# Moving the weight scans' fetches to GpSimd's queue, with five buffers for the last eight, in a four-layer linear-attention and gated-MLP kernel

## The chip, the cores and the metric

The kernel runs on one core of a Trainium2 chip. The metric is the device time of one execution in microseconds (us). Before the change it was 1498.74 us (median of three runs, 1498.54 to 1498.86). All runs named below gave correct results.

## The reference

Layer A is linear attention and layer B a gated MLP without a nonlinearity. The program applies A, B, A, B with the same weights.

```python
def A(x, wqkv, wo):                       # S=2048, D=1024, 32 heads of 32
    q, k, v = split_heads(x @ wqkv)
    phi = lambda t: where(t > 0, t + 1, exp(t)) + 1e-6
    pq, pk = phi(q), phi(k)
    kv, z = einsum("bhsd,bhse->bhde", pk, v), einsum("bhsd->bhd", pk)
    o = einsum("bhqd,bhde->bhqe", pq, kv) / (einsum("bhqd,bhd->bhq", pq, z)[..., None] + 1e-6)
    return merge_heads(o) @ wo

def B(x, w_gate, w_up, w_down):           # F=3584
    return ((x @ w_gate) * (x @ w_up)) @ w_down

x = x + A(layernorm(x)); x = x + B(layernorm(x)); x = x + A(layernorm(x)); x = x + B(layernorm(x))
```

## The kernel before

The kernel computes layer B in float16, so it needs one power-of-two scale per weight matrix. During the first layer A it therefore *scans* `w_gate`, `w_up` and `w_down`: 42 pieces of 512 KB are fetched, and ScalarE squares and sums each (L221). Pieces 0 to 27 are gate and up, and 28 to 41 are down. The first 14 fetches are issued by the sync engine, the other 28 by ScalarE itself, most of them right after the scan that frees their buffer.

```python
scan_a = [K[i][:, j * 2 * D:(j + 1) * 2 * D] for i in (3, 1) for j in range(2)]
scan_b = [W[:, 6 * D:8 * D], K[0][:, HEAD:HEAD + 2 * D]]
scan_c = [K[i][:, HEAD:HEAD + 2 * D] for i in (4, 0)]
# ... cut ...
EARLY, MID = 26, 33
scan_buf = [scan_a[i % 4] for i in range(18)] + [(scan_a + scan_b[:1])[i % 5] for i in range(18, EARLY)]
scan_buf += [scan_b[(i + 1) % 2] for i in range(MID - EARLY)] + [scan_c[i % 2] for i in range(NSCAN - MID)]

def scan_fetch():
    while scanned[1] < scanned[2]:
        i = scanned[1]
        if any(scan_buf[j] is scan_buf[i] for j in range(scanned[0], i)):
            return                                   # buffer not scanned yet
        src, k = scan_src(i)
        (nc.sync if i < 14 else nc.scalar).dma_start(                                        # L213
            out=scan_buf[i].rearrange("p (k n) -> p k n", k=k), in_=src)
        scanned[1] += 1

def scan_step(n=1):
    for _ in range(n):
        i = scanned[0]                                   # cut: the indices of acc
        nc.scalar.activation(out=scan_buf[i], in_=scan_buf[i], func=ACT.Square, accum_out=acc[...])   # L221
        scanned[0] += 1
        # ... cut: loads of wv, and the limit raised to MID ...
        scan_fetch()

def scale_sum(lo, hi):      # VectorE: L230 sums acc into part, L231 copies it to partb
def scale_pow(lo, hi):      # TensorE: one-column matmul with ones (L236); VectorE max; GpSimd power (L238)
def scale_bits(lo, hi):     # VectorE: keep the exponent only
```

The stage with the change is the second half of layer A. Eleven `q` tiles are woven with products `pk^T x` (`xk`). Then come `kv_unit` (L490), five more `q` tiles with `kvo_unit` between them (the products with `wo`, L500), and 16 output tiles (L510, with VectorE's add to `X` at L512). Each slot of the output stage carries *jobs* for the other engines: norms for layer B, the scans left over, the scale chain of `w_down`, and the preparation of layer B's weights.

```python
def kvo_unit(c):
    def run():
        ps = turn("kvo", QP[2:4])
        for n in range(2):
            nc.tensor.matmul(out=ps[:, n, :], lhsT=kvt[:, c, :], rhs=wo[n][:, c, :], start=True, stop=True)
        nc.scalar.activation(out=KVo[c], in_=ps, func=ACT.Copy, scale=rz[:, c:c + 1])
    return run
# ... cut ...
for t in range(XT_):                                  # XT_ = 11
    q_tile(t, li > 0, done=2 * (t < XT_ - 1))
    do(rest[pos[0]:pos[1]])                           # xk products
    # ... cut: z, and the scale chain of gate and up at t = 7, 8, 9 ...
    if t == XT_ - 3:
        load_o()                                      # wo, two halves, sync queue
    scans(0 if t > 8 else 2 - t % 2)
kv_unit()
load_unit(0, 0)
if first_A:
    scanned[2] = NSCAN
    scan_fetch()                                      # the last pieces of w_down: two buffers
q_tile(XT_, True)
# ... cut ...
    job(13, lambda: scale_sum(2, 3))
    job(13, dp[1][0])
    job(17, lambda: scale_pow(2, 3))
    job(19, lambda: scale_bits(2, 3))
    for i in range(2, 11):
        job(i, scans)
    for i, f in enumerate(list(dp[0][1:]) + list(dp[1][1:])):
        job((20, 21, 26, 27)[i], f)                   # dp: prepared w_down, stored to DRAM as WD
```

Of the kernel before, what the change touches and what calls it, by code (L numbers as in the profile page):

```python
# [37 lines left out]
def kernel(  # L38
# [11 lines left out]
    nc = tc.nc  # L50
    P = 128
    S, D = A_x.shape[1], A_x.shape[2]
# [27 lines left out]
    K = [const.tile([P, BLK], BF16, tag=f"K{i}", name=f"K{i}") for i in range(8)]  # L80
# [3 lines left out]
    QP = [QQ[:, 2 * i:2 * i + 2, :] for i in range(4)]  # L84
    WD = dram.tile([7, P, BLK], F16, name="WD")

    HEAD = KD * NB
# [22 lines left out]
    kvt = W[:, 5 * D:6 * D].rearrange("p (c f) -> p c f", f=P)  # L110
    scan_a = [K[i][:, j * 2 * D:(j + 1) * 2 * D] for i in (3, 1) for j in range(2)]
    scan_b = [W[:, 6 * D:8 * D], K[0][:, HEAD:HEAD + 2 * D]]
    scan_c = [K[i][:, HEAD:HEAD + 2 * D] for i in (4, 0)]

    xn_c = {TPG + i: tail(i, 0) for i in range(4)}
    xn_b = [ST[:, t % TPG * D:(t % TPG + 1) * D] for t in range(NT)]
# [8 lines left out]
    def turn(name, bufs):  # L125
        count[name] = count.get(name, -1) + 1
        return bufs[count[name] % len(bufs)]
# [70 lines left out]

    NGU = 2 * NU
    NSCAN = 3 * NU  # L200
    EARLY, MID = 26, 33
    scan_buf = [scan_a[i % 4] for i in range(18)] + [(scan_a + scan_b[:1])[i % 5] for i in range(18, EARLY)]
    scan_buf += [scan_b[(i + 1) % 2] for i in range(MID - EARLY)] + [scan_c[i % 2] for i in range(NSCAN - MID)]
    scanned = [0, 0, 0]

    def scan_fetch():

        while scanned[1] < scanned[2]:
            i = scanned[1]
            if any(scan_buf[j] is scan_buf[i] for j in range(scanned[0], i)):  # L210
                return
            src, k = scan_src(i)
            (nc.sync if i < 14 else nc.scalar).dma_start(out=scan_buf[i].rearrange("p (k n) -> p k n", k=k), in_=src)  # L213
            scanned[1] += 1

    def scan_step(n=1):
# [12 lines left out]
    def scale_sum(lo, hi):  # L229
        nc.vector.tensor_reduce(out=part[:, lo:hi], in_=acc[:, lo:hi, :], axis=AX.X, op=ALU.add)  # L230
        nc.vector.tensor_copy(out=partb[:, lo:hi], in_=part[:, lo:hi])  # L231

    def scale_pow(lo, hi):

        ps = mm_tile()
        nc.tensor.matmul(out=ps[:, lo:hi], lhsT=ones[:], rhs=partb[:, lo:hi], start=True, stop=True)  # L236
        nc.vector.tensor_scalar(out=part[:, lo:hi], in0=ps[:, lo:hi], scalar1=1e-30, scalar2=None, op0=ALU.max)
        nc.gpsimd.tensor_tensor(out=fac[:, lo:hi], in0=part[:, lo:hi], in1=mhalf[:, lo:hi], op=ALU.pow)  # L238
# [30 lines left out]
    def ln_stats(t):  # L269
        bn(t, 0)  # L270
        bn(t, 1)
        moments(t)
# [222 lines left out]
    def kvo_unit(c):  # L495

        def run():
            ps = turn("kvo", QP[2:4])
            for n in range(2):
                nc.tensor.matmul(out=ps[:, n, :], lhsT=kvt[:, c, :], rhs=wo[n][:, c, :], start=True, stop=True)  # L500
            nc.scalar.activation(out=KVo[c], in_=ps, func=ACT.Copy, scale=rz[:, c:c + 1])
        return run
# [181 lines left out]
    def layer_A(li):  # L684
        sks = [sum_unit(t, nc.vector) for t in range(1, NT)]
        first_A = li == 0

        def scans(n=1):
            if first_A:
                scan_step(n)  # L690

        if li == 0:
            def txp(t):
                return lambda: tx_pe(xn_a[t], t)

            def norm(t):
                ln_apply_act(t, xn_a[t])
                tx(xn_a[t], t, t // TPG)

            bn(0, 0)  # L700
            bn(0, 1)
            moments(0)
            bn(1, 0)
            bn(1, 1)
            ln_tx_halves(0, xn_a[0])
            ln_apply(1, xn_a[1])
            ln_stats(2)
            u = k_mm(0, 0, txp(1), KD // 2)
            ln_apply(2, xn_a[2])
            phi(*u)  # L710
            u = k_mm(1, 0, txp(2))
            ln_stats(3)
            bn(4, 0)
            ln_apply(3, xn_a[3])
            bn(4, 1)
            moments(4)
            phi(*u)
            ln_apply(4, xn_a[4])
            tx(xn_a[4], 4, 1)

            units = [(2, 0), (0, 1), (1, 1), (3, 0), (2, 1), (3, 1)]
            units += [(t, n) for t in range(TPG, NT) for n in range(2)]
            ready = []
            for i, (t, n) in enumerate(units):
                if t < TPG:
                    u = k_mm(t, n, txp(3), KD // 2) if i == 1 else k_mm(t, n)
                elif n == 0:
                    u = k_tile(t)
                late = ready
                ready = [4 + (i + 4) // 2 if i > 1 else 5 + i] if i < 2 or (i % 2 == 0 and i <= 18) else []  # L730
                for x in ready:
                    ln_stats(x)
                if t < TPG or n == 0:
                    phi(*u)
                for x in late:
                    norm(x)
                if i == 2:
                    for x in range(3 * TPG, NT):
                        load_x(x)
                if i >= 5 and i % 2:  # L740
                    scanned[2] = (i - 3) // 2 if i < len(units) - 1 else EARLY
                    scan_fetch()
                if 10 <= i <= 28 and i % 2 == 0:
                    scans()
                if t > 10 and n == 1:
                    sks.pop(0)()
            load_qkv(wq, 0)
        else:
            load_qkv(wq, 0)
            load_qkv(wv, 2)  # L750
            count["mm"] = 5
            fill = norm_fill(3, 3, xn_a)
            for t in range(NT):
                phi(*k_tile(t), True)
                do(fill[2 * t:2 * t + 2])
                if t > 0:
                    sks.pop(0)()

        xk = [xk_pair(c) for c in range(KD)]
        first = 3 if first_A else 1  # L760
        for i in range(first):
            xk[i]()
            do(sks[5 * i:5 * i + 5])
            if i == min(2, first - 1):
                z_parts()
            scans(3)
        rest = xk[first:]
        XT_ = 11

        for t in range(XT_):  # L770
            pos = [-(-len(rest) * x // (XT_ - 1)) for x in (t, t + 1)]
            q_tile(t, li > 0, done=2 * (t < XT_ - 1))
            do(rest[pos[0]:pos[1]])
            if t == 0:
                z_unit()
            elif t == 2:
                z_column()
            elif first_A and t == 7:
                scale_sum(0, 2)
            elif first_A and t == 8:  # L780
                scale_pow(0, 2)
            elif first_A and t == 9:
                scale_bits(0, 2)
            if t == XT_ - 3:
                load_o()
            scans(0 if t > 8 else 2 - t % 2)
        kv_unit()
        load_unit(0, 0)
        if first_A:
            scanned[2] = NSCAN  # L790
            scan_fetch()
        q_tile(XT_, True)
        norm = norm_act(0, 0, xn_b, TPG) + norm_act(1, 1, xn_c, 2)
        late = norm[10:]
        jobs = {i: norm[i - 8:i - 7] for i in range(8, 18)}
        for i in range(6):
            jobs[18 + i] = late[len(late) * i // 6:len(late) * (i + 1) // 6]

        def job(i, *f):
            jobs[i] = list(f) + jobs.get(i, [])  # L800

        for i in range(4):
            job(3 + i, prep(0)[i])
        if first_A:
            job(9, dp[0][0])
            job(13, lambda: scale_sum(2, 3))
            job(13, dp[1][0])
            job(17, lambda: scale_pow(2, 3))
            job(19, lambda: scale_bits(2, 3))
            for i in range(2, 11):  # L810
                job(i, scans)
            for i, f in enumerate(list(dp[0][1:]) + list(dp[1][1:])):
                job((20, 21, 26, 27)[i], f)
        job(24, lambda: load_unit(1, 1))
        for i in range(4):
            kvo_ = [kvo_unit(2 * i), kvo_unit(2 * i + 1)]
            q_tile(XT_ + 1 + i, True, kvo_[0:1], kvo_[1:2], 2)
        count["mm"] = 7
        for t in range(NT):
            if t == NT - 2:  # L820
                load_unit(2, 2)
                if first_A:
                    dp[2][0]()
                sums_t[:] = t_fill()
            if t in (7, 10, 13) and not (first_A and t == 10):
                mm_pair()
            out_tile(t)
            if t < 3:
                flush()
                flush()  # L830
            do(jobs.get(2 * t, []))
            do(jobs.get(2 * t + 1, []))
            if t >= NT - 2:
                sums_t.pop(0)()
# [215 lines left out]
```

## Time and profile before

| | before |
|---|---|
| median, first three runs | 1498.74 us |
| TensorE (PE) busy | 1478.4 of 1497.5 us |
| wait of PE for the scale of `w_down` | 3.57 us, then 4 us at a reduced clock |
| wait of ScalarE for the last fetches | 1.38 and 4.33 us |

The profile is of a run of 1499.30 us. PE is busy for 99% of the span, so only its gaps can be won. This is the list of PE's waits between 100 and 260 us. A row reads: engine, line, what it waited for, total us, times, longest.

```profile
PE Q L236 <- DVE partb L231: 3.6, 1, 3.6
PE Q L372 <- DVE W L364: 0.8, 1, 0.8
PE Q L500 <- ACT W L359: 0.4, 1, 0.4
PE Q L510 <- DVE X L512: 0.4, 1, 0.4
PE Q L500 <- DMA TX<-in_A_wo_dram: 0.3, 1, 0.3
```

The first row is the largest. PE's timeline (start, duration, engine, line, operation; in brackets the idle time before it and what ended it) shows it in place:

```profile
217.76 1.67 PE L510 MATMUL Q<-K,K 128*128 128x512 bf16 x7
223.00 0.16 PE L236 MATMUL Q<-partb,ones 128*128 128x1 bf16 x1 [3.57 <-DVE partb L231]
223.03 5.28 PE L510 MATMUL Q<-K,K 128*128 128x512 bf16 x15
```

Fifteen matmuls take 5.28 us after the gap, while seven took 1.67 us before it. The windows table says why. After each window stand its length, the busy time of each engine, and at the end three figures without a count: PE's granted clock, the DMA share and GB/s.

```profile
core 0: us, PE busy (x) PEld busy (x) DVE busy (x) ACT busy (x) POOL busy (x), PEclk, DMA share, GB/s
219.00:223.00 4.00, 0.43 (x3) 0.10 (x1) 0.38 (x3) 4.00 (x7) 0.21 (x1) 1.00 0.58 183
223.00:225.00 2.00, 2.00 (x6) 0.73 (x6) 2.00 (x2) 2.00 (x5) 1.07 (x4) 0.50 0.49 187
225.00:227.00 2.00, 2.00 (x6) 0.77 (x6) 0.27 (x2) 2.00 (x4) 0.96 (x4) 0.64 0.00 0
```

The clock falls to 0.50 and 0.64 for two windows of 2 us: 1.0 + 0.7 = 1.7 us more. ScalarE's timeline shows what made the sum late:

```profile
207.75 1.91 ACT L221 ACTIVATE K<-K 128x2048 bf16<-128x2048 bf16 x1 [1.38 <-DMA K<-in_B_w_down_dram]
...
214.08 1.91 ACT L221 ACTIVATE K<-K 128x2048 bf16<-128x2048 bf16 x1 [4.33 <-DMA K<-in_B_w_down_dram]
...
220.57 1.89 ACT L221 ACTIVATE K<-K 128x2048 bf16<-128x2048 bf16 x1
```

With two buffers, a fetch can leave only after a scan, and the last scan ends at 222.5 us. Between 126 and 160 us ScalarE stands still for 2.5 us in all behind five of its own issues.

### The profile page before, as it was taken

To read this page: it belongs to the slowest core of one execution; us is meant where nothing else is said; L and a number is where in the kernel's file an instruction comes from. 1 tells how busy PE (TensorE), PEld (TensorE's weight loads), DVE (VectorE), ACT (ScalarE), POOL (GpSimd) and SP (SyncE) were. 2 spreads that over 40 slices of the span, in tenths; PEclk is the share of its full clock that TensorE was granted. 3 is DMA by queue.
4 is the path that set the end of the run, shared out by engine and by line. 5 is a ranking of instruction groups with operands and counts; after the bars stand their busy time and mean duration, and the time that the engine had idled before them with its cause. 6 is when DMAs were issued, how large, how long until landed. Compare 5 with 4: busy or idle time off the path is not lost. (4 is left out here: it accounts for less than half of the span.)

```text
span 1497.5 us, 17477 instructions
## 1 busy us (share of the span) xinstructions
PE 1478.4 (99%) x6895; PEld 676.3 (45%) x6997; DVE 1007.7 (67%) x1426; ACT 709.6 (47%) x650; POOL 68.3 (5%) x178
## 2 busy tenths in 40 slices
PE   8999989999999999999999999999999999999999
PEld 3444434444444444444444445444444444444444
DVE  7847877888865477767385357767776845777532
ACT  4986676877601366640045326546554015666200
POOL 2100002000000000001020000200000100000000
PEclk9999999999999999999999999999999999999999
DMA  7876677677657333336560015343332763333442
GB/s 214 223 238 166 172 169 176 200 206 212 199 181 190 85 85 85 86 126 191 167 169 0 14 29 127 64 106 92 96 94 100 214 186 99 85 84 85 151 168 82
DMA packets 276818, 202.74 MB, mean 135 GB/s; under 512 B 101760, under 2 KB 264064, under 8 KB 273152
## 3 DMA queue, kind: packets, MB, share of 16 engines
q1 hardware_dynamic: 265392, 186.81, 44.5%
q10 hardware_dynamic: 11344, 14.81, 3.2%
q8 instruction: 55, 0.90, 0.2%
q14 instruction: 27, 0.22, 0.0%
HBM read 160.43 MB, written 17.04 MB: 119 GB/s over the span
## 5 line engine op out<-in xcount | busy, mean ns | idle before, releaser
L576 PEld LDWEIGHTS <-K 128*128 128x128 f16 x3136 | 306.8, 98 | 370.0
L576 PE MATMUL Q<-XT,K 128*128 128x512 bf16 (+1 forms) x1734 | 394.5, 379 | 3.1
L871 PE MATMUL Q<-K,K 128*128 128x512 f16 (+2 forms) x1582 | 340.4, 377 | 0.0
L576 PE MATMUL Q<-TX,K 128*128 128x512 f16 x1344 | 308.4, 379 | 0.0
L538 ACT ACTIVATE K<-K,fac 128x2048 f16<-128x2048 bf16 x112 | 224.7, 2009 | 129.1 <-DMA K<-in_B_w_gate_dram 128.2
L871 PEld LDWEIGHTS <-K 128*128 128x128 f16 x1582 | 154.3, 98 | 184.5
L541 DVE TENSOR_TENSOR K<-K 128x1024 f16<-128x1024 f16 (+1 forms) x244 | 157.0, 666 | 102.6 <-ACT K L538 100.7
L355 ACT ACTIVATE W<-Q 128x1024 bf16<-128x1024 f32 (+1 forms) x68 | 65.8, 970 | 148.5 <-PE Q L372 143.6
L541 DVE TENSOR_TENSOR W<-MX,Q 128x1024 f16<-128x1024 f32 x88 | 107.4, 1221 | 38.4 <-PE Q L576 19.5
L596 ACT COPY MX<-Q 128x1024 f32<-128x1024 f32 x60 | 60.8, 1013 | 122.4 <-PE Q L576 110.1
L372 PE MATMUL Q<-K,XT 128*128 128x512 bf16 x497 | 112.8, 379 | 3.0 <-DMA XT<-ST 0.9
L372 PE MATMUL Q<-K,K 128*128 128x512 bf16 x502 | 113.2, 379 | 0.5
L541 DVE TENSOR_TENSOR W<-W,Q 128x1024 f16<-128x1024 f32 x80 | 97.6, 1221 | 17.9 <-PE Q L576 13.2
L596 ACT COPY W<-Q 128x1024 f32<-128x1024 f32 x52 | 52.7, 1013 | 92.9 <-PE Q L576 79.9
L541 DVE TENSOR_TENSOR K<-K,K 128x512 f16<-128x512 f16 (+1 forms) x148 | 87.6, 597 | 4.2
L360 DVE TENSOR_SCALAR W<-W 128x1024 bf16<-128x1024 bf16 (+1 forms) x68 | 27.5, 404 | 83.5 <-ACT W L355 83.4
L372 PEld LDWEIGHTS <-XT 128*128 128x128 bf16 x512 | 49.4, 98 | 62.2 <-DMA XT<-ST 1.4
L372 PEld LDWEIGHTS <-K 128*128 128x128 bf16 x512 | 49.9, 98 | 60.3 <-issue 0.6
L580 DVE TENSOR_TENSOR K<-W 128x512 f16<-128x512 f16 x168 | 71.4, 425 | 5.8
L221 ACT ACTIVATE K<-K 128x2048 bf16<-128x2048 bf16 x37 | 70.6, 1907 | 9.9 <-DMA K<-in_B_w_down_dram 5.7
L258 DVE BATCH_NORM_STATS2 st<-X 128x6 f32<-128x512 bf16 x104 | 65.8, 674 | 2.4 <-DMA X<-in_A_x_dram 2.3
L885 DVE SCALAR_TENSOR_TENSOR W<-Q,kap,X 128x1024 f32<-128x1024 f32 x16 | 20.5, 1284 | 65.8 <-PE Q L871 65.8
(121 smaller groups left out, 1131.6 us busy)
## 6 DMA issues: line engine op xcount, KB each, us to landing
K<-WD SPq DMA_DIRECT2D x28, 1792.0 KB, 7.4
K<-in_B_w_gate_dram SPq DMA_DIRECT2D x70, 512.0 KB, 4.1
K<-in_B_w_up_dram SPq DMA_DIRECT2D x56, 512.0 KB, 5.2
K<-in_A_wqkv_dram SPq DMA_DIRECT2D x10, 1024.0 KB, 7.8
K<-in_B_w_down_dram ACTq DMA_DIRECT2D x12, 512.0 KB, 4.2
K<-in_B_w_up_dram ACTq DMA_DIRECT2D x11, 512.0 KB, 4.0
K<-in_B_w_down_dram SPq DMA_DIRECT2D x10, 512.0 KB, 5.4
WD<-K SPq DMA_DIRECT2D x10, 512.0 KB, 3.0
```

Source lines behind the costliest of these rows:

```text
L221: nc.scalar.activation(out=scan_buf[i], in_=scan_buf[i], func=ACT.Square, accum_out=acc[:, m, c:c + 1])
L258: nc.vector.bn_stats(out=stat[t][0][:, c, :], in_=X[:, t, c * NB:(c + 1) * NB])
L355: nc.scalar.activation(out=e, in_=ps, func=ACT.Exp)
L360: nc.vector.tensor_scalar(out=e, in0=e, scalar1=1.0, scalar2=1e-6, op0=ALU.min, op1=ALU.add)
L372: nc.tensor.matmul(out=ps, lhsT=xt[:, k, tl * P:(tl + 1) * P], rhs=w[:, k, :], start=(k == 0), stop=(k == KD - 1))
L538: nc.scalar.activation(out=b.bitcast(F16), in_=b, func=ACT.Copy, scale=fac[:, m:m + 1])
L541: eng.tensor_tensor(out=o, in0=a, in1=b, op=op)
L576: nc.tensor.matmul(out=pair[:, m, :], lhsT=stationary(n, p, m, k), rhs=moving[p][:, k, :], start=(p in (1, 2, 5) and k == 0), stop=(k == K ...
L580: nc.vector.tensor_tensor(out=hA[i][:, u, :], in0=gu[:, 0, :], in1=gu[:, 1, :], op=ALU.mult)
L596: nc.scalar.copy(out=snaps[u, p], in_=a)
L871: nc.tensor.matmul(out=ps_[:, lo:hi], lhsT=act[:, u, j * P:(j + 1) * P], rhs=w[:, u, lo:hi], start=(p in (1, 2, 5) and u == 0), stop=(u == ...
L885: stt(out=o, in0=ps_, scalar=kap[:, 0:1], in1=x, op0=ALU.mult, op1=ALU.add)
```

## The change

The intent is to end the late sum. GpSimd is idle from 57 to 217 us but for one operation, so it issues the fetches. The last eight scans get five buffers, which are filled well ahead of the output stage. The sum, the power and the exponent of the scale chain are spread over more slots. Fewer scans stand ahead of the first `q` tiles, and the two PSUM pairs of `kvo` are swapped.

```diff
-    scan_c = [K[i][:, HEAD:HEAD + 2 * D] for i in (4, 0)]
+    scan_c = [K[i][:, HEAD:HEAD + 2 * D] for i in (4, 0, 1, 2, 3)]
-    EARLY, MID = 26, 33
+    EARLY, MID = 26, 34
-    scan_buf += [... [scan_c[i % 2] for i in range(NSCAN - MID)]
+    scan_buf += [... [scan_c[i % 5] for i in range(NSCAN - MID)]
-            (nc.sync if i < 14 else nc.scalar).dma_start(...)
+            (nc.sync if i < 14 else nc.gpsimd).dma_start(...)
-            ps = turn("kvo", QP[2:4])
+            ps = turn("kvo", [QP[3], QP[2]])
-            scans(3)
+            scans(3 if i < 2 else 2)
     # scale chain of gate and up: power and bits one q tile later (t = 9, 10)
-            scans(0 if t > 8 else 2 - t % 2)
+            scans((1, 2, 2, 2, 2, 2, 2, 2, 1, 0, 0)[t])
         kv_unit()
         load_unit(0, 0)
-        if first_A:
-            scanned[2] = NSCAN
-            scan_fetch()
         q_tile(XT_, True)
     # jobs: scale_sum 13 -> 14, scale_pow 17 -> 18, scale_bits 19 -> 21, dp (20, 21, 26, 27) -> (22, 23, 26, 27)
-            for i in range(2, 11):
+            for i in range(1, 9):
                 job(i, scans)
         for i in range(4):
             kvo_ = [...]
             q_tile(XT_ + 1 + i, True, kvo_[0:1], kvo_[1:2], 2)
+            if first_A and i == 0:
+                scanned[2] = NSCAN
+                scan_fetch()
```

Scans 14 to 25 have four or five buffers, before and after. Scans 26 to 33 (26 to 32 before) have two (`scan_b`).

More of the change, by code (lines that the diff above doesn't have):

```diff
@@ L200 @@
     NSCAN = 3 * NU
-    EARLY, MID = 26, 33
+    EARLY, MID = 26, 34
     scan_buf = [scan_a[i % 4] for i in range(18)] + [(scan_a + scan_b[:1])[i % 5] for i in range(18, EARLY)]
-    scan_buf += [scan_b[(i + 1) % 2] for i in range(MID - EARLY)] + [scan_c[i % 2] for i in range(NSCAN - MID)]
+    scan_buf += [scan_b[(i + 1) % 2] for i in range(MID - EARLY)] + [scan_c[i % 5] for i in range(NSCAN - MID)]
     scanned = [0, 0, 0]
@@ L212, in scan_fetch @@
             src, k = scan_src(i)
-            (nc.sync if i < 14 else nc.scalar).dma_start(out=scan_buf[i].rearrange("p (k n) -> p k n", k=k), in_=src)
+            (nc.sync if i < 14 else nc.gpsimd).dma_start(out=scan_buf[i].rearrange("p (k n) -> p k n", k=k), in_=src)
             scanned[1] += 1
@@ L779, in layer_A @@
                 scale_sum(0, 2)
-            elif first_A and t == 8:
+            elif first_A and t == 9:
                 scale_pow(0, 2)
-            elif first_A and t == 9:
+            elif first_A and t == 10:
                 scale_bits(0, 2)
@@ L805, in layer_A @@
             job(9, dp[0][0])
-            job(13, lambda: scale_sum(2, 3))
+            job(14, lambda: scale_sum(2, 3))
             job(13, dp[1][0])
-            job(17, lambda: scale_pow(2, 3))
-            job(19, lambda: scale_bits(2, 3))
-            for i in range(2, 11):
+            job(18, lambda: scale_pow(2, 3))
+            job(21, lambda: scale_bits(2, 3))
+            for i in range(1, 9):
                 job(i, scans)
             for i, f in enumerate(list(dp[0][1:]) + list(dp[1][1:])):
-                job((20, 21, 26, 27)[i], f)
+                job((22, 23, 26, 27)[i], f)
         job(24, lambda: load_unit(1, 1))
```

## The prediction

> **What bounds the kernel.** TensorE: the page shows PE busy 1478.4 of 1497.5 us (99%), VectorE 67%, ScalarE 47%, GpSimd 5%. Only PE's gaps can be won. The list of PE's waits sums to about 11 us; in the stage that changes:
>
> - 3.57 us at 219.4 us: the one-column matmul of the scale chain waits for `partb`. The timeline shows why: ScalarE's last scans of `w_down` waited 1.38 and 4.33 us for their fetches (two buffers, each refetched only after its scan), the last scan ended at 222.5 us, and VectorE idled 8.0 us before the sum.
> - Directly after it the windows table shows a granted clock of 0.50 from 223 to 225 us and 0.64 from 225 to 227, against 1.00 before and after: 1.0 + 0.7 = 1.7 us of lost matmul time. The Trainium skill ("TensorE: Matmul & The Clock Gate", Part 1) says that PE falls to half clock after an idle window of about 3.4 us; this trace agrees with its 3.57 us gap.
> - 0.39 + 0.28 us at 171.1 us: the first `kvo` matmuls wait for the bank that the last `phi` still reads, then for the second half of `wo`, which landed 11.0 us after issue, beside two scan fetches.
> - 0.79 us at 102.6 us (phi late behind scans on ScalarE), 0.38 us at 212 us.
>
> **What the change does.** Some 28 fetches leave ScalarE's queue, where each cost about 0.45 us of ScalarE's time. They go to GpSimd, idle from 57 to 217 us but for one 0.7 us operation. The last eight scans have five buffers; their fetches depend only on the last `xk` reads and on GpSimd's own power operation, so I expect five issued around 165 to 171 us and landed before the first is scanned at about 190. The last scans then run back to back: 8 x 2.0 us plus two converts of 2.0 us from 190.8, done at about 211 instead of 222.5. The sum now stands after output tile 7 (about 216 us) and its matmul after tile 9 (about 222): several us of slack. The stall goes, and its clock dip too. Fewer scans before the first two q tiles should remove most of the 0.79. The swapped `kvo` bank and the later scan fetches should remove about half of 0.67.
>
> **Sum.** 3.6 + 1.7 (if the prefetch works) + 0.6 + 0.4 = 6.3 us, all on PE, so all on the critical path. VectorE has idle time to follow (8.0 + 3.1 us before), so I expect no new wait at layer B.
>
> **Predicted: 1492.4 us, range 1490.4 to 1496.0. Faster by over 2%: 0.005; within 2%: 0.985; slower by over 2%: 0.01.**
>
> **What would show it.** PE's wait for `partb` gone, granted clock 1.00 throughout 220 to 230 us; last scan ended by 213 us with no wait for DMA; no queue-issue gaps on ScalarE; layer B's first product at about 243 us instead of 248.9; second half of `wo` landed by about 171 us.
>
> **What would make it wrong.** GpSimd's fetches land later: the skill ("DMA: Bandwidth & Descriptors", latency table) gives about 1 us to the first byte against 0.6 us; no trace here shows it. With two buffers between scans 26 and 33 ScalarE could then wait, delay `phi` and open new PE gaps. Or the five early fetches crowd `wo` and make `kvo` wait up to 3 us.

## More of the kernel before

The sync queue's timeline gives the moment at which the second half of `wo` is issued. It stands behind a transpose out of `W` in program order, which is issued at 159.40 us:

```profile
161.31 0.64 SPq L146 DMA_DIRECT2D TX<-in_A_wo_dram  x1
```

## The result, and the profile after

Ratios here and below are the mean time of one kernel's runs over that of the other's of the same rounds, so they are not quite the ratio of the medians that are quoted. All outputs are right.

| | before | after |
|---|---|---|
| median of six runs | 1498.80 us | 1496.62 us |
| range | 1497.39 to 1500.72 | 1493.83 to 1500.28 |
| ratio | | 0.9987, 95% interval 0.9968 to 1.0005 |

Two groups of runs stand behind the median of after: 1493.83, 1494.75 and 1494.76 at a mean granted clock of 1.000, and 1498.48, 1499.58 and 1500.28 at 0.999. The profile is of the 1494.76 us run, with a span of 1492.9 us.

What was expected of the late sum happened. PE no longer waits for `partb`, and its clock stays at 1.00. First PE's timeline of after, then its windows:

```profile
217.69 5.56 PE L510 MATMUL Q<-K,K 128*128 128x512 bf16 x25
223.09 0.17 PE L236 MATMUL Q<-partb,ones 128*128 128x1 bf16 x1
```

```profile
219.00:223.00 4.00, 4.00 (x20) 1.85 (x19) 1.22 (x1) 2.57 (x4) 0.29 (x2) 1.00 0.39 76
223.00:225.00 2.00, 2.00 (x12) 0.90 (x10) 1.29 (x2) 0.00 (x0) 0.34 (x1) 1.00 0.59 111
225.00:227.00 2.00, 2.00 (x11) 0.87 (x9) 0.23 (x1) 0.58 (x1) 1.14 (x4) 1.00 0.00 0
```

GpSimd issues the five fetches in one piece, and ScalarE's last eight scans run back to back. GpSimd's timeline, then ScalarE's last scan, with nothing in brackets:

```profile
167.32 3.61 POOL L213 DMA_DIRECT2D K<-in_B_w_down_dram  x5
```

```profile
207.50 1.90 ACT L221 ACTIVATE K<-K 128x2048 bf16<-128x2048 bf16 x1
```

But PE's list of waits for the same stretch, 100 to 260 us, has other rows now:

```profile
PE Q L500 <- DMA TX<-in_A_wo_dram: 1.4, 1, 1.4
PE Q L510 <- DVE X L512: 1.0, 1, 1.0
PE Q L576 <- DVE TX L541: 0.9, 1, 0.9
```

The wait for `wo` was to shrink, and it grew. The wait for VectorE's add grew from 0.4 to 1.0 us, and one for `TX` opened. ScalarE's waits between 126 and 160 us and the sync queue's timeline show something new upstream:

```profile
ACT K L221 <- DMA K<-in_B_w_down_dram: 6.9, 3, 5.2
ACT K L398 <- PE Q L396: 3.6, 1, 3.6
ACT W L221 <- DMA W<-in_B_w_down_dram: 1.4, 2, 0.9
```

```profile
163.71 0.63 SPq L146 DMA_DIRECT2D TX<-in_A_wo_dram  x1
```

ScalarE now waits 6.9 + 1.4 = 8.3 us for fetches of scans in the two-buffer stretch, where it waited for none. `wo` is issued 2.4 us later than before (163.71 against 161.31), again behind that transpose (161.80). It lands faster, 8.3 us after issue against 11.0, so in all 0.3 us earlier; but PE arrives 1.4 us earlier (172.03 - 1.42 = 170.61 against 172.33 - 0.28 = 172.05) and waits.

The same matmul placed in both traces gives the ledger (start after minus start before, cumulative). At `kv_unit` PE is 0.88 us ahead, because the 0.79 us wait is gone. At the second half of the first `kvo` it is 0.30 ahead, and at 212.7 us it is 0.36 behind. At layer B's first product it is 5.02 ahead (243.84 against 248.86); at the product that waits for `TX`, 3.98 ahead; at the end, 4.6. The stall and the clock dip are thus worth 5.4 us, as predicted, and new waits take some of it back. The 0.6 us between `TX` and the end are spread over the remaining 1240 us and were not attributed.

Why did PE's lead of 0.30 us turn into a lag of 0.36 by 212.7 us? There VectorE sets the pace. In both traces it works without a gap from about 188 to 214 us, and PE waits for its add. In after these adds run 0.37 us later, since VectorE had stood idle for 0.75 us before 187.70 us until a transpose out of `MX` was done. VectorE's timeline, before and then after:

```profile
211.10 3.47 DVE L512 TENSOR_TENSOR X<-X,Q 128x1024 bf16<-128x1024 bf16 x3
```

```profile
211.47 3.47 DVE L512 TENSOR_TENSOR X<-X,Q 128x1024 bf16<-128x1024 bf16 x3
```

In all twenty profiles PE waits for an add of VectorE in this stage, so what PE gains ahead of it is lost again unless VectorE comes earlier too. None of this yet explains the slower group of runs.

### The profile page after: what moved, and what is told of

The parts are those of the page before. It is cut to its first block, busy times and chain, and to the rows that moved or that the text cites. A ratio compares the mean times of both kernels' runs of the same rounds, so it can differ in the third digit from the quotient of the medians.

```text
span 1492.9 us, 17625 instructions
## 1 busy us (share of the span) xinstructions
PE 1482.9 (99%) x6997; PEld 676.0 (45%) x6997; DVE 1008.1 (68%) x1426; ACT 707.9 (47%) x650; POOL 89.9 (6%) x206
## 3 DMA queue, kind: packets, MB, share of 16 engines
q0 software_dynamic: 4032, 14.68, 3.2%
## 5 line engine op out<-in xcount | busy, mean ns | idle before, releaser
L576 PE MATMUL Q<-XT,K 128*128 128x512 bf16 (+1 forms) x1792 | 405.7, 379 | 0.0
L372 PE MATMUL Q<-K,XT 128*128 128x512 bf16 x512 | 113.5, 379 | 1.4 <-DMA XT<-ST 0.8
L372 PE MATMUL Q<-K,K 128*128 128x512 bf16 x512 | 114.1, 379 | 0.0
L372 PEld LDWEIGHTS <-K 128*128 128x128 bf16 x512 | 50.0, 98 | 61.4 <-issue 1.7
L372 PEld LDWEIGHTS <-XT 128*128 128x128 bf16 x512 | 49.4, 98 | 61.2 <-DMA XT<-ST 1.3
```

Source lines behind the costliest of these rows:

```text
L372: nc.tensor.matmul(out=ps, lhsT=xt[:, k, tl * P:(tl + 1) * P], rhs=w[:, k, :], start=(k == 0), stop=(k == KD - 1))
L576: nc.tensor.matmul(out=pair[:, m, :], lhsT=stationary(n, p, m, k), rhs=moving[p][:, k, :], start=(p in (1, 2, 5) and k == 0), stop=(k == K ...
```

## The experiments

All runs used five rounds beside the kernel before on the same chip. The texts on record name their theories by letters, which belong to their own call. Three questions had to be told apart. (1) Do the gains come from the buffers, the queue or the spacing of the jobs? (2) Is the loss due to *when* the late fetches crowd `wo`, or to *which queue* carries the fetches of the two-buffer stretch? (3) What makes the slower group?

| label | edit in short | median us (range) | ratio, 95% interval | before, same chip |
|---|---|---|---|---|
| again | changed kernel | 1498.57 (1494.06 to 1502.19) | 0.9995, 0.9978 to 1.0013 | 1498.86 |
| act_queue | changed kernel, ScalarE's queue | 1493.61 (1493.20 to 1493.95) | 0.9965, 0.9953 to 0.9977 | 1498.86 |
| queue_only | before, GpSimd's queue | 1496.15 (1494.22 to 1497.10) | 0.9979, 0.9967 to 0.9991 | 1498.86 |
| jobs_only | before, jobs spread | 1500.46 (1499.09 to 1502.78) | 1.0013, 1.0000 to 1.0025 | 1498.86 |
| gp_gate | changed, late fetches gated | 1496.23 (1493.76 to 1501.17) | 0.9987, 0.9972 to 1.0003 | 1499.12 |
| act_early | ScalarE's queue, late fetches early | 1502.54 (1501.19 to 1503.89) | 1.0020, 1.0008 to 1.0032 | 1499.12 |
| act_oldjobs | ScalarE's queue, jobs of before | 1492.44 (1492.26 to 1492.74) | 0.9954, 0.9943 to 0.9966 | 1499.12 |
| mixed | GpSimd 14 to 33, ScalarE last eight | 1496.22 (1495.12 to 1498.12) | 0.9980, 0.9968 to 0.9992 | 1499.12 |
| own_bufs | changed, own buffers for four q tiles | 1494.36 (1494.08 to 1500.63) | 0.9981, 0.9966 to 0.9995 | 1498.66 |
| late_gp_gate | ScalarE 14 to 33, GpSimd last eight, gated | 1493.63 (1492.89 to 1494.35) | 0.9966, 0.9954 to 0.9977 | 1498.66 |
| buffers_only | before, five buffers | 1493.64 (1493.24 to 1494.17) | 0.9966, 0.9954 to 0.9978 | 1498.66 |
| best | act_oldjobs and own_bufs | 1492.66 (1492.04 to 1493.25) | 0.9959, 0.9946 to 0.9971 | 1498.66 |
| gp_14_25 | changed, GpSimd for 14 to 25 only | 1492.99 (1492.68 to 1493.21) | 0.9966, 0.9953 to 0.9978 | 1497.59 |
| gp_26_33 | changed, GpSimd for 26 to 33 only | 1494.19 (1493.35 to 1494.40) | 0.9972, 0.9959 to 0.9984 | 1497.59 |
| best_a | gp_14_25, jobs of before | 1491.83 (1491.55 to 1492.10) | 0.9958, 0.9944 to 0.9971 | 1497.59 |
| again2 | changed kernel | 1494.52 (1492.96 to 1497.17) | 0.9974, 0.9961 to 0.9986 | 1498.19 |
| gp_26_33b | repeat of gp_26_33 | 1494.61 (1494.05 to 1496.87) | 0.9977, 0.9964 to 0.9989 | 1498.19 |
| best_a2 | repeat of best_a | 1492.23 (1491.47 to 1492.88) | 0.9956, 0.9943 to 0.9970 | 1498.19 |

### Does the spread repeat? (again)

The edit is a comment only.

> The changed kernel once more, unchanged, to see whether its two groups of times (1494 and 1499 us) come back. Theory A (a PE gap that on some executions or chips grows [...] brings a clock dip back): runs fall in two groups about 4 us apart, and a slow one shows a granted clock under 1.00 for about 3 us somewhere between 160 and 260 us. Theory B (a property of the chip or of the session, not of the change): all runs of one chip agree within 1 us and the kernel before on the same chip is slower by 4 to 5 us in every round.

The two groups came again: 1494.06, 1494.27, then 1498.46 to 1502.19. The profile fell on the 1502.19 us run. There `wo` is issued at 164.66 us and PE waits 1.99 us for it. The sync queue then spends 7.16 us on issuing one load of `w_up` (2.65 us in after) and 14.10 us on two transposes out of `MX` behind it (11.00 us), and at 193.46 us VectorE has stood idle for 5.16 us until one of them is done (0.75 us). It stays behind in the output stage, where PE waits for its adds four times, 5.0 us in all. One of these gaps is 2.31 us long, and after it the granted clock reads 0.90, 0.50 and 0.75 in the three windows of 2 us from 218 to 224 us. A late chain thus costs its waits and, when one gap is long enough, a clock dip of 0.2 + 1.0 + 0.5 = 1.7 us. What made the chain late is asked below.

### The queue alone taken back (act_queue)

```diff
-            (nc.sync if i < 14 else nc.gpsimd).dma_start(...)
+            (nc.sync if i < 14 else nc.scalar).dma_start(...)
```

> The changed kernel with its scan fetches back on ScalarE's queue, all else kept. If the five buffers and the spacing do the work, the wait for partb stays away and the time is within 1 us of the changed kernel; ScalarE shows its 0.45 us gaps again, the first fetches for the last scans issue about 173 us instead of 167 and the wait for the second half of wo falls from 1.42 to under 0.5 us. If GpSimd's queue is what matters, the wait for partb comes back with 2 us or more.

The changed kernel without GpSimd's queue is steady, at 1493.61 us with a range of 0.75 us. On the same chip the changed kernel itself (again) took 1498.57 us, and no run of it was as fast as the slowest of act_queue. So GpSimd's queue made the changed kernel slower. PE does not wait for `wo`. ScalarE's waits between 126 and 160 us and the issue of `wo` read:

```profile
ACT K L221 <- DMA K<-in_B_w_down_dram: 4.2, 2, 3.5
...
ACT W L221 <- DMA W<-in_B_w_down_dram: 0.3, 1, 0.3
```

```profile
162.63 0.63 SPq L146 DMA_DIRECT2D TX<-in_A_wo_dram  x1
```

ScalarE waits 4.5 us instead of 8.3, and `wo` leaves 1.1 us earlier. The 3.8 us less of waiting are not all gain, as ScalarE's own issues cost it gaps again. The scans show the net. The scan that frees the first late buffer starts at 129.94 us in after and 130.26 here, and the last scan of the stretch at 157.45 and 156.40, so the chain is 1.4 us longer through GpSimd. On this route the 2.4 us by which `wo` was late come in two steps, 1.3 us with all of the change but GpSimd's queue (161.31 to 162.63) and 1.1 us with that too (to 163.71). The placement of the scans is the likely cause of the first, as with the buffers alone `wo` leaves at 161.09 us (buffers_only). The next run shows that these steps don't simply add.

### The queue alone, on the kernel before (queue_only)

```diff
-            (nc.sync if i < 14 else nc.scalar).dma_start(...)
+            (nc.sync if i < 14 else nc.gpsimd).dma_start(...)
```

> The kernel before with only the queue changed: scan fetches from GpSimd. My theory (two buffers are the cause of the late last scan): the wait for partb stays at 3 us or more, since GpSimd's fetches land no sooner (5.7 to 9.4 us median in the changed kernel's trace against 4.0 to 4.2), and the time is 1498 to 1501 us. Rival (ScalarE's queue delays the scans): the wait shrinks under 1.5 us and the time falls to about 1495.

My expectation was that the stall would stay at 3 us or more, and it missed: PE's wait for `partb` shrank to 1.41 us, and no clock dip follows, because ScalarE's last scan now ends at about 218.8 us. In the last scans GpSimd's queue helps with two buffers. Over the whole kernel it is worth 2.7 us at the median, with a range of 2.9 us.

This run also bears on the stretch between 126 and 160 us. There GpSimd fetches scans 26 to 32 in this run, ScalarE waits 2.4 us for them, and yet `wo` leaves 1.9 us *earlier* than in the kernel before (161.31). The sync queue's timeline of queue_only:

```profile
159.44 0.63 SPq L146 DMA_DIRECT2D TX<-in_A_wo_dram  x1
```

So two buffers and GpSimd's queue alone do not make `wo` late. It takes another part of the change too, most likely the placement of the scans, which puts 16 instead of 14 of them into the first nine `q` tiles and so leaves less time for each fetch. GpSimd's queue with five buffers and the old placement was not run.

### The spacing of the jobs alone (jobs_only)

```diff
-            job(13, lambda: scale_sum(2, 3))
+            job(14, lambda: scale_sum(2, 3))
-            job(17, lambda: scale_pow(2, 3))
+            job(18, lambda: scale_pow(2, 3))
-            job(19, lambda: scale_bits(2, 3))
+            job(21, lambda: scale_bits(2, 3))
-                job((20, 21, 26, 27)[i], f)
+                job((22, 23, 26, 27)[i], f)
```

> The kernel before with only the scale chain and the two preparations that follow it moved one output tile later, buffers and queue as before. If the stall is only a question of where the matmul stands: one more output tile is 3.45 us of PE work, so the 3.57 us wait shrinks to 0 to 0.8 us, no clock dip follows, and the time is 1493 to 1495 us, as good as the whole change. If the fetches are what matters, the wait stays above 2 us.

I expected 1493 to 1495 us and got 1500.46. The wait for `partb` is gone, but it did not vanish. It moved 20 us down the line, because ScalarE's norms come as late as before (the last starts at 240.07 us against 240.53), and VectorE stands behind them: it is idle for 2.83 and 1.67 us until GpSimd, which serves those norms first, has the `rstd` of VectorE's own. PE's timeline and one window:

```profile
242.76 5.30 PE L510 MATMUL Q<-K,K 128*128 128x512 bf16 x16 [2.64 <-DVE X L512]
```

```profile
245.00:247.00 2.00, 2.00 (x6) 0.72 (x5) 2.00 (x4) 0.00 (x0) 0.00 (x0) 0.50 1.03 295
```

A gap of 2.64 us brings the clock dip back as well. Giving a late value more room does not make it less late.

### The buffers alone (buffers_only)

```diff
+    scan_c = [K[i][:, HEAD:HEAD + 2 * D] for i in (4, 0, 1, 2, 3)]      # in kernel before
+    ... [scan_c[i % 5] for i in range(NSCAN - MID)]
     # and the last scan_fetch() moved from behind kv_unit to behind the first kvo, ScalarE's queue
```

> The kernel before with only the five buffers for the last scans (nine of them here), fetched from ScalarE's queue at the first kvo as in act_queue; queue, scan counts, kvo bank and the scale chain as before. If the buffers alone cure the stall: no DMA wait on ScalarE after 188 us, last scan by 213 us, no wait for partb above 0.5 us, no clock dip, 1493 to 1494.5 us. If the moved scans are needed too, the wait for partb stays above 1 us.

The kernel before with five buffers takes 1493.64 us, a ratio of 0.9966, the same as act_queue. PE does not wait at the scale's matmul:

```profile
218.59 0.17 PE L236 MATMUL Q<-partb,ones 128*128 128x1 bf16 x1
```

The 0.8 and 0.4 us waits at L372 and `kvo` stay, as this version does not touch them. The buffers and their issue moment, which were moved together, bring 5.0 us alone (1498.66 to 1493.64).

### Is it the moment of the late fetches? (gp_gate, act_early)

In the changed kernel GpSimd issues the five fetches at 167.3 to 170.9 us, while `wo` is on its way; ScalarE's queue issued them at 173.6. A tiny GpSimd copy that reads the first `kvo` result holds them back:

```diff
+                gate = const.tile([P, 1], BF16, tag="gate", name="gate")
+                nc.gpsimd.tensor_copy(out=gate[:], in_=KVo[0][:, 0, 0:1])
                 scanned[2] = NSCAN
                 scan_fetch()
```

> The changed kernel, still fetching from GpSimd, but a one-column copy on GpSimd that reads the first kvo block stands before the five early fetches, so that they go out at about 173.5 us, when ScalarE's queue sent them in act_queue, instead of at 167.3. Theory T (the moment matters: five fetches of 512 KB beside wo, the two unit loads and the transposes make those late): wo's second half no longer stalls PE (under 0.5 us instead of 1.4 to 2.0), the transposes out of MX land within 10 us, VectorE's wait for them is gone, and all runs lie between 1492.5 and 1495. Theory K (GpSimd's kind of queue itself makes the transposes late): two groups of times remain, some runs above 1498, and VectorE waits several us for the transposes out of MX.

The fetches now leave at 173.7 us, yet PE waits 1.36 us for `wo` and the spread stays (1493.76 to 1501.17). The second half of `wo` is still issued at 163.58 us, and ScalarE still waits 8.4 us for fetches in 126 to 160 (the profile is of a 1494.95 us run). That the moment of the five late fetches alone is the cause falls.

The opposite case puts the five fetches ahead of `wo`, on ScalarE's queue:

```diff
         load_unit(0, 0)
+        if first_A:
+            scanned[2] = NSCAN
+            scan_fetch()
         q_tile(XT_, True)          # and removed behind the first kvo; queue scalar
```

> The other corner: fetches from ScalarE's queue, but the five early ones sent before the last q tile, at about 162 us. Theory T: wo's second half is late again (PE waits 1.5 to 3 us), VectorE waits for the transposes out of MX, and runs above 1496 appear. Theory K: as good as act_queue, 1493 to 1494.5 in all runs.

It is the slowest version, 1502.54 us. PE waits 1.27 us for the first half of `wo` and 6.07 us for the second:

```profile
178.61 0.58 PE L500 MATMUL Q<-TX,W 128*128 128x512 bf16 x1 [6.07 <-DMA TX<-in_A_wo_dram]
```

So the moment can cost a great deal. In the changed kernel a later moment brought nothing (gp_gate), so this was not its main trouble.

### Which stretch of fetches is it? (mixed, late_gp_gate)

mixed keeps GpSimd for scans 14 to 33 and gives the last eight to ScalarE. late_gp_gate does the reverse, with the gate.

```diff
 # mixed
+            (nc.sync if i < 14 else nc.gpsimd if i < MID else nc.scalar).dma_start(...)
 # late_gp_gate
+            (nc.sync if i < 14 else nc.scalar if i < MID else nc.gpsimd).dma_start(...)
```

> The changed kernel with fetches 14 to 33 from GpSimd and only the last eight from ScalarE's queue. Theory T: stable like act_queue, and it keeps what the GpSimd queue gave in the q tiles (PE there 0.9 us ahead of the kernel before): 1492.5 to 1494. Theory K (GpSimd fetches make runs unstable wherever they are): two groups again, some runs above 1497.

> The complement of mixed: fetches 14 to 33 on ScalarE's queue, the last eight on GpSimd's, released by the first kvo block as in gp_gate. If GpSimd's fetches in the two-buffer stretch (scans 26 to 33) are what starts the delay, this is as steady as act_queue, 1493 to 1494.5, wo issued by 162.6 us with no PE wait above 0.5 us. If GpSimd's five fetches beside the transposes are enough by themselves, VectorE waits for the transposes out of MX and some runs lie above 1497.

| median us | last eight: ScalarE | last eight: GpSimd, gated |
|---|---|---|
| scans 14 to 33: ScalarE | 1493.6 (act_queue) | 1493.6 (late_gp_gate) |
| scans 14 to 33: GpSimd | 1496.2 (mixed) | 1496.2 (gp_gate) |

The row decides and the column does not. Both cells of the second row ran on one chip and those of the first on two others, so only the large difference is read. The chip is not the reason: act_oldjobs on the second row's chip was steady at 1492.44 us, and on act_queue's chip the changed kernel was the slow one. GpSimd is a good issuer for the last eight scans with five buffers. It costs about 2.6 us somewhere in scans 14 to 33.

### Which part of 14 to 33? (gp_14_25, gp_26_33, on one chip)

```diff
 # gp_14_25
+            (nc.sync if i < 14 else nc.gpsimd if i < EARLY else nc.scalar).dma_start(...)
 # gp_26_33
+            (nc.sync if i < 14 else nc.gpsimd if EARLY <= i < MID else nc.scalar).dma_start(...)
```

> The changed kernel with GpSimd's queue for fetches 14 to 25 only (four or five buffers), ScalarE's for all later ones. If the two-buffer stretch is where GpSimd's later landing hurts, this is as steady as act_queue: 1493 to 1494.5, ScalarE's waits for fetches between 126 and 160 us sum to about 4.5 us as there, wo issued by 162.6 us. If fetches 14 to 25 are the cause, the spread of mixed (1495 to 1498) comes back.

> GpSimd's queue for fetches 26 to 33 only (two buffers in turn). If the two-buffer stretch is the cause: ScalarE's waits for fetches between 126 and 160 us sum to 8 us or more, wo issues at 163 us or later, and the times spread like mixed or wider, 1494.5 to 1500, median over 1495. If not, 1493 to 1494.5.

ScalarE's waits between 126 and 160 us and the issue of `wo`, first gp_14_25, then gp_26_33:

```profile
ACT K L221 <- DMA K<-in_B_w_down_dram: 4.1, 2, 3.6
```

```profile
162.05 0.63 SPq L146 DMA_DIRECT2D TX<-in_A_wo_dram  x1
```

```profile
ACT K L221 <- DMA K<-in_B_w_down_dram: 7.4, 3, 5.1
```

```profile
163.54 0.63 SPq L146 DMA_DIRECT2D TX<-in_A_wo_dram  x1
```

With GpSimd for 14 to 25, where four or five buffers stand, ScalarE waits 4.1 us, the second half of `wo` leaves at 162.05 us, and PE does not wait for it. With GpSimd for 26 to 33, where two buffers stand, ScalarE waits 8.0 us (7.4, and 0.6 for the other buffer), `wo` leaves at 163.54, and PE waits 1.30 us. The medians differ by 1.2 us, and the ranges do not touch. That places the loss in the two-buffer stretch, at the changed placement of the scans. That the number of buffers is what makes this stretch sensitive is not shown: it was never raised there, and the stretch also has transposes and `wo` beside it. And gp_26_33 was to show the wide spread and did not (1493.35 to 1494.40), a partial miss.

### The slower runs: a buffer shared with VectorE? (own_bufs, best)

In the slow profile of again VectorE waited for a buffer in `MX`, which is in use until its transpose has left. own_bufs gives `q` tiles 12 to 15 buffers of their own.

```diff
-        pq = turn("pq", pqb)
+        pq = tail(7, t - 12) if 12 <= t < 15 else tail(6, 0) if t == 15 else turn("pq", pqb)
```

> The changed kernel, GpSimd's queue and early fetches kept, but q tiles 12 to 15 write their phi into four blocks of their own (tails of K6 and K7 that stand free), so VectorE need not wait until the transposes have read the MX blocks. In the slow execution caught in the run called again, VectorE waited 5.16 us there, and PE then lost 5.0 us in four waits for X plus 1.7 us of clock. If that wait is what makes the slow group: VectorE's wait for a transpose out of MX is gone in every trace, the runs above 1498 vanish, and all lie between 1492.5 and 1496 (wo's late second half, 1.4 to 2.0 us, stays). If the slow runs come from elsewhere, the two groups stay.

> act_oldjobs (ScalarE's queue, five buffers, chain in its old place; 1492.4) with the four own blocks of own_bufs. In act_oldjobs VectorE did not wait for the transposes, so I expect no more than 0.3 us from it: 1492.0 to 1492.7, and no run above 1493.

VectorE's wait for transposes out of `MX` is gone, but slow runs stay (1497.49 and 1500.63 beside 1494.08 to 1494.52). The profile fell on the 1497.49 us run: PE waits 2.61 us for `MX` at 161.41 us, ahead of the tiles that the edit touches, after ScalarE waited 4.18 us for the fetch that was issued at 149.15. In best, own_bufs adds nothing to act_oldjobs (1492.66 on its chip, against 1492.44 on another), and one run of 1493.25 lies above the bound set for it. Shared buffers are not what makes the slow runs.

### Does the spread belong to the kernel or to the chip? (again2, gp_26_33b, on one chip)

> The changed kernel unchanged, on one chip with the next run. On the chip of the last call the version that sends only scans 26 to 33 from GpSimd was steady (1493.4 to 1494.4), but the changed kernel did not run beside it. Theory K (the spread belongs to the kernel: fetches of both stretches from GpSimd): this run shows two groups again, 1493.8 to 1495 and 1498 to 1502, median above 1495, while the next run on the same chip stays within 1493 to 1495. Theory C (the spread depends on the chip or on chance at the start, not on which scans GpSimd fetches): both runs are alike, both spread or both steady within 1.5 us. In either case the ScalarE waits for fetches between 126 and 160 us should sum to about 8 us or more.

> Repeat of the version that sends only scans 26 to 33 from GpSimd, beside the changed kernel. Theory K: steady, 1493 to 1495, and clearly under the changed kernel (by 1.5 us or more in the median). Theory C: within 1 us of the changed kernel's median and with the same spread. Both expect the wait of TensorE for the second half of wo at 1.2 us or more.

On this chip both are alike: 1494.52 and 1494.61 us, with ranges of 4.2 and 2.8 us. Theory K falls in this form: fetches of 26 to 33 alone spread as the full change does, and how far they spread differs (gp_26_33: 1.05 us). The wait for `wo`, expected at 1.2 us or more in both, was 1.1 us in gp_26_33b and absent in again2, where PE itself was late.

The profile of again2 caught a slow run early in its course. It is the 1497.17 us run. Four timelines of again2 follow in order of time: the fetch by GpSimd, the scan on ScalarE, the first operation on VectorE, and PE.

```profile
148.65 0.70 POOL L213 DMA_DIRECT2D K<-in_B_w_down_dram  x1 [2.11 <-ACT K L221]
```

```profile
156.07 1.91 ACT L221 ACTIVATE K<-K 128x2048 bf16<-128x2048 bf16 x1 [4.16 <-DMA K<-in_B_w_down_dram]
```

```profile
159.02 0.43 DVE L360 TENSOR_SCALAR W<-W 128x1024 bf16<-128x1024 bf16 x1 [4.70 <-ACT W L355]
```

```profile
160.81 4.03 PE L372 MATMUL Q<-K,K 128*128 128x512 bf16 x12 [2.80 <-DVE MX L364]
```

In after, the same fetch left at almost the same time and its scan started 3 us sooner:

```profile
148.49 0.70 POOL L213 DMA_DIRECT2D K<-in_B_w_down_dram  x1 [1.80 <-ACT K L221]
```

```profile
153.12 1.91 ACT L221 ACTIVATE K<-K 128x2048 bf16<-128x2048 bf16 x1 [1.12 <-DMA K<-in_B_w_down_dram]
```

The fetch took 7.4 us to its scan (156.07 - 148.65) against 4.6. ScalarE stands still until it lands, so the exponential of the next `q` tile is late, then VectorE's part of `phi`, and then PE, which needs that PSUM bank. Its gap is 2.80 us, and the clock falls again, as again2's windows show:

```profile
162.00:164.00 2.00, 2.00 (x7) 0.73 (x5) 1.90 (x4) 0.70 (x1) 0.00 (x0) 0.53 0.00 0
164.00:166.00 2.00, 2.00 (x7) 0.73 (x6) 1.91 (x3) 0.00 (x0) 0.00 (x0) 0.62 0.02 4
```

That is 0.9 + 0.8 = 1.7 us of clock on top of the gap. In own_bufs the same fetch was the late one, issued at 149.15 us and landed 7.5 us later. In the slow profile of again it landed 4.9 us after its issue at 149.20, and it was the load of `w_up` and the transposes that were late (see above). Two transposes out of `W` start to be issued beside this fetch at nearly the same time (148.64 us in after, 148.50 in again2, 149.06 in own_bufs), so their issue time is not what differs.

### The version that the experiments point to (act_oldjobs, best_a, best_a2)

act_oldjobs is act_queue with the job slots of the kernel before (the reverse of the diff of jobs_only); best_a adds GpSimd for scans 14 to 25.

> act_queue with the scale chain and the preparations back in the places of the kernel before (sum after tile 6, matmul after tile 8). If the early fetches alone end the stall, the last scan ends at about 210 us, the sum is ready by 214 us, the matmul at about 218.5 us does not wait, and the time is 1493 to 1494. The stores of the prepared w_down blocks then stand before the last four transposes again, as in the kernel before, so the 0.7 us wait for the sums into TX at layer B's start may go, which would make it 0.5 us faster than act_queue. If the spacing of the chain matters, the wait for partb comes back with over 1 us.

> act_oldjobs with GpSimd's queue for fetches 14 to 25 only. If those are harmless and free ScalarE of its 0.45 us gaps before the first q tiles: 1492.0 to 1492.8, no run above 1493.3, not clearly faster than act_oldjobs (1492.4).

> Repeat of the best version on another chip: GpSimd fetches scans 14 to 25 only, ScalarE's queue the rest, five buffers, jobs of the kernel before. Expected 1491.5 to 1493 with a range of under 1 us, ratio to the kernel before 0.995 to 0.997, whichever theory holds. If it spreads to 1498 or above, neither theory's account of what starts the slow executions stands.

act_oldjobs takes 1492.44 us, better than the 1493 to 1494 expected of it. That this is the time predicted for the change itself is chance, as it leaves out the move to GpSimd and the new slots. The comparison of the slots on one chip is best_a against gp_14_25: 1491.83 against 1492.99, with ranges apart. So the new spacing of the jobs costs 1.2 us. The sync queue's timelines show how. After, then act_oldjobs:

```profile
233.36 4.08 SPq L308 DMA_TRANSPOSE XT<-K  x2
237.53 1.11 SPq L138 DMA_DIRECT2D WD<-K  x2
238.75 3.95 SPq L308 DMA_TRANSPOSE XT<-K  x2
```

```profile
229.34 0.92 SPq L138 DMA_DIRECT2D WD<-K  x2
230.36 6.80 SPq L308 DMA_TRANSPOSE XT<-K  x4
```

With the later slots the stores of the prepared `w_down` stand between the last four transposes. The last ones leave at up to 242.7 us instead of 237.2, and the first `TX` sum of layer B starts at 244.79 instead of 239.86. This is the 0.9 us wait of PE for `TX`, which act_oldjobs and best_a do not have. (The slots are not its only source: queue_only has the old ones and waits 0.75 us there.) GpSimd for 14 to 25 adds nothing that can be told from zero (ratios 0.9954 without it, 0.9958 and 0.9956 with it). best_a came out a little under its expectation (1491.83), and best_a2 spread by 1.41 us where under 1 us was expected. best_a beats the kernel before on both chips on which it ran; on the second one the changed kernel ran too, at 1494.52 us against 1492.23.

## Why the prediction was wrong where it was wrong

The result was within 2% as expected, but the median, 1496.62 us, lies 0.6 us above the range of 1490.4 to 1496.0 and 4.2 above the predicted 1492.4. Term by term of its sum:

- **"3.6 + 1.7 (if the prefetch works)": right.** The wait and the clock dip are gone (0 us, clock 1.00), the ledger jumps by 5.4 us there, and layer B starts at 243.84 us as said ("about 243"). buffers_only shows that the five buffers, with their later issue, do this alone. The last scan ended at 209.5 us, inside the predicted 213.
- **"Most of the 0.79": right, but it did not arrive.** It is gone, and the ledger shows a lead of 0.88 us at `kv_unit`, but a lag of 0.36 us at 212.7.
- **"All on PE, so all on the critical path": wrong for what PE gains before 212 us.** PE waited for VectorE there already (0.38 us), and in after VectorE came 0.37 us later. The gains of 0.6 + 0.4 ended as a loss of 0.36 us.
- **"The swapped `kvo` bank and the later scan fetches should remove about half of 0.67": wrong.** The 0.39 for the bank is gone, but the wait for `wo` grew from 0.28 to 1.42 us. This is a loss of 0.75 us in place of a gain of 0.4. The reason given, that the fetches would stay out of `wo`'s way, held for the transfer, which took 8.3 us instead of 11.0, but the wait had another end: `wo` itself was issued 2.4 us later, and landed at 172.0 instead of the predicted 171. gp_gate moved the fetches behind `wo` and the wait stayed. GpSimd's queue made it late only together with the rest of the change, most likely the placement of the scans; alone it made `wo` 1.9 us earlier (queue_only).
- **"No new wait at layer B": wrong.** PE waits 0.89 us for `TX`. VectorE did have idle time: it stood still for 2.51 us before that sum, which reads transposes that the sync queue issued late. This comes with the job slots, which the prediction counted as pure slack.
- **The step that failed most is "GpSimd, idle from 57 to 217 us".** An idle issuer was read as a free move, but in the changed kernel this move cost 5.0 us at the median on one chip (1498.57 in again against 1493.61 in act_queue). ScalarE is spared about 0.45 us per fetch, but what counts where the next scan stands waiting is the time from one scan's end to the next landing. Through GpSimd ScalarE waits about 8 us between 126 and 160 us (eight profiles of five-buffer versions with fetches 26 to 33 on that queue: 8.0 to 10.8), through its own queue 4.1 to 4.7 (eight profiles), all at the changed placement of the scans. At the old placement it is 2.4 us through GpSimd (queue_only) and 0 through ScalarE (before, buffers_only). The prediction named this among what could make it wrong ("with two buffers between scans 26 and 33 ScalarE could then wait, delay `phi` and open new PE gaps"), but gave it no weight in the sum.
- **The range had no place for two groups of runs.** Eight builds of five-buffer versions that fetch scans 26 to 33 on ScalarE's queue, with the last fetches behind `wo`, all stay within 1.5 us. Of the eight with GpSimd in that stretch, all but one spread by 2.8 us or more. But GpSimd is not the only way to a spread: the kernel before, all on ScalarE's queue and with a long PE gap, spread by 2.1 to 4.1 us on the five chips of the experiments. In the slow runs whose profile was caught, one transfer lands later still (the scan's fetch by up to 3 us in again2 and own_bufs, transposes in again), PE's longest gap is 2.3 to 2.8 us, and the clock dip adds 1.7 us. Without the slow group the median would have been 1494.75, which is inside the range.

It stays open why transfers land so differently between executions of one kernel when GpSimd issues the fetches of the two-buffer stretch. The queue table shows that GpSimd's fetches travel in larger packets: 4032 packets for 14.68 MB, or 3.6 KB each, against 11344 for 14.81 MB, or 1.3 KB, on ScalarE's queue. No run changed the packet size, so this is a hint and no cause. The Trainium skill ("DMA: Bandwidth & Descriptors", section "Issuing engines are not separate DMA queues") says that transfers run on the same 16 engines whoever starts them, so that another issuer only saves issue time. The results agree in part: in ratio to the kernel before, no version of the changed kernel with fetches moved to GpSimd was clearly faster than its counterpart on ScalarE's queue. On the kernel before, the move did gain 2.7 us (queue_only).

## What to carry to other kernels

Before moving a fetch to an idle engine's queue, look at the chain from one use of a buffer to the next: where the reader already waits for the refill, every tenth of a microsecond from release to landing is added to the chain, and the idle issuer may lengthen it (1.4 us over one stretch, in one pair of profiles here). The same move helped where the reader had slack. Five buffers, filled ahead of their use, gave most of the gain here (5.0 us of the 5.8 to 6.7 of the best versions). A gain on the busiest engine counts only as far as the next point where it waits for another. Work that waits behind a late value should not be given later slots before it is known who stands behind it in the same queue; and in this kernel the five gaps of TensorE of 2.3 to 3.6 us that the traces show cost about 1.7 us more than themselves.

## What the Trainium skill lacked or had wrong

- "TensorE: Matmul & The Clock Gate", Part 1, gives an idle window of about 3.4 us as what halves the clock, and says that the window runs freely. Here the granted clock fell to 0.50 to 0.53 in a window of 2 us after gaps of 2.31, 2.61, 2.64 and 2.80 us too, as well as after 3.57 and within one of 6.07; after gaps of 1.42, 1.81 and 1.99 us it did not. In these cases a gap of two thirds of the stated window was enough.
- "DMA: Bandwidth & Descriptors", section "Latency and other measured facts", gives the first byte at about 1 us through GpSimd and 0.6 us through the hardware queues. The fast runs agree roughly: three fetches for which ScalarE waits in both traces took 7.7, 4.6 and 5.2 us from issue to scan through GpSimd (after) and 6.9, 4.1 and 5.0 through ScalarE (act_queue). The level and the spread are what the page lacks. Its fit in "Anatomy of one DMA — SWDGE (gpsimd) path", 2.0 us plus bytes over 436 GB/s, gives an estimate of 3.2 us for 512 KB. Here GpSimd's 512 KB fetches beside transposes and other loads took 3.9 to 7.7 us from the start of issue to the start of the scan that waited for them (after, between 126 and 160 us), and the same fetch of the same program took 4.6 us in one execution and 7.4 in another. No page gives a spread between executions of one program.
- No page gives the issuer's cost of one such fetch: 0.70 to 0.76 us of GpSimd's time (0.97 for the first, in after), and 0.37 to 0.53 us of ScalarE's queue (in before) with a gap of about 0.45 us in its work.
